# Loads, gains and first norms of the opening quads: which queue issues them and in which order

## The chip, the cores and the metric

The kernel runs on one core of one Trainium2 chip. A core has five engines with a queue of instructions each: TensorE (PE, matrix products and transposes), VectorE (DVE), ScalarE (ACT), GpSimd (POOL) and SyncE (SP, which here only issues DMA transfers). Every engine takes its own queue strictly in order and waits on semaphores for the others. The metric is device time in microseconds (us), the median of several executions. The profile is of one further execution.

## The reference

Attention with normalised queries and keys, followed by a feed-forward block with SoLU. The inputs are float32, but for the two weight matrices: these are float64, and the kernel reads them as pairs of 32-bit words.

```python
q_n = q / sqrt(mean(q*q, -1) + 1e-6) * g_q          # (8, 12, 448, 64); the same for k with g_k
scores = q_n @ k_n.T / 8
attn = exp(scores - max); attn = attn / (sum(attn) + 1e-9)
x = (attn @ v) as (3584, 768)
h = x @ w_in                                         # (768, 1024)
solu = h * softmax(h)
ln = (solu - mean) / sqrt(var + 1e-6) * g_ln
out = ln @ w_out                                     # (1024, 768)
```

## The kernel before

The 8 batches of 12 heads are 48 *pairs* of heads, and two pairs make a *quad*; there are 24 quads. The attention runs over them in one loop, with the order of every engine's work written out by hand (`tc.manual_schedule()`); the two products of the feed-forward block follow, with the block sums of a fast matrix multiplication. The change touches the set-up before the loop, and quad 0.

A quad m with pairs a and b goes through these steps. `scores(n, kc)` makes the scores for 128 of a pair's 448 keys on TensorE (L802) and an exponential `E` of them on ScalarE (L792), called E(n,kc) below; `scores_last(m)` does the remaining 64 keys of both pairs (L815). `add(n)` sums two of the exponentials on VectorE to `es` (L829). `values_last`, `values` multiply by v, `sums` makes the row sums of the exponentials on TensorE from `E` and `es` (L874), and `inverse` and `divide` end the quad on VectorE and GpSimd. Between them stand the preparations of later pairs: `squares` (ScalarE, L656), `row_sums` (VectorE, L664), `fold_one` or `fold_sums`, `rsqrt_seed` (Ln and Exp on ScalarE), `rsqrt_step` (four VectorE instructions of a Newton step), `normalise` (GpSimd, L713), `qk_transpose` (VectorE, L723) and `gain` (ScalarE, L727).

Pairs 0 and 1 are loaded by rows (`load_rows`, L738) and are transposed by TensorE: `square_rows` (L748, L750), `sum_rows` (L756), `rsqrt_seed`, `rsqrt_step` (L694 to L704), `normalise_rows` (the scaling, L764), `transpose_rows` (L770) and `take_rows` (L776, L778), the copy out of PSUM in which ScalarE multiplies q by the gain column `gcol`. All later pairs come through `load` (L634), eight transfers of 56 KB each. `load_gains` (L465 to L472) fetches the vectors g_q and g_k broadcast over the partitions (`gg`), once more as two rows, and g_ln (`grow`); `gain_columns` (L479 to L481) transposes the rows to `gcol` and multiplies the two broadcasts, `gain_limit` makes the factor of the q column from them.

The DMA transfers of both issuing queues take eight completion semaphores in turn, and each one waits until the transfer that last had its semaphore has landed. Before the loop SP issues, in this order: q of pair 0 (k goes over ScalarE's queue at the same time), the six transfers of the gains, pair 1, pair 2, v of quad 0, pairs 3, 4 and 5. In quad 0 SP goes on with v of quad 1 and pairs 6 and 7. Much later, in the first product of the feed-forward block, ScalarE's queue issues loads too (`load_x`, L924), and GpSimd's power serves the layer norm (L1050), one column at a time; L1052 is a scale and multiply of one column there.

Of the kernel before, what the change touches and what calls it, by code (L numbers as in the profile page):

```python
# [9 lines left out]
FP32 = mybir.dt.float32  # L10
# [4 lines left out]
OP = AluOpType  # L15
# [351 lines left out]
def fast_path(  # L367
# [24 lines left out]
    nc = tc.nc  # L392
    B, H, S, D = q.shape
    DM, DFF = moe_w_in.shape
    P = 128
    NJ = S // P
    NB = S // 32
# [64 lines left out]

    def load_gains():
        for i, g in enumerate((g_q, g_k)):
            nc.sync.dma_start(gg[:, i], g.rearrange("(o d) -> o d", o=1).to_broadcast([P, D]))  # L465
        for i, g in enumerate((g_q, g_k)):
            nc.sync.dma_start(
                grow[KF + i : KF + i + 1].rearrange("o (h d) -> o h d", h=2),
                g.rearrange("(o d) -> o () d", o=1).to_broadcast([1, 2, D]),
            )  # L470
        for i in range(2):
            nc.sync.dma_start(  # L472
                grow[i * HF : (i + 1) * HF].rearrange("c (g j) -> c g j", g=4),
                moe_g_ln.rearrange("(h g c j) -> h c g j", h=2, g=4, j=32)[i],
            )
# [148 lines left out]

    def load(n):
        b, hp = divmod(n, NP)
        h0 = 2 * hp
        d = st[n] = {}  # L630
        d["qk"] = loads.tile([P, 2, NB, 32], FP32, tag="qk", name="qk", bufs=5)
        for s, src in enumerate((q, k)):
            for g in range(4):
                nc.sync.dma_start(  # L634
                    d["qk"][g * 32 : g * 32 + 32, s],
                    src[b, h0 + g // 2].rearrange("(b t) (x d) -> x t b d", t=32, x=2)[g % 2],
                )
# [104 lines left out]
    def square_rows(n, s, engine):  # L742
        d = st[n]
        if s == 0:
            d["sq"] = xs.tile([P, 2, 4, P], FP32, tag="x", name="xsq")[0:R]
        x, y = d["qk"][:, s], d["sq"][:, s]
        if engine is nc.scalar:
            nc.scalar.activation(y, x, AF.Square)  # L748
        else:
            engine.tensor_tensor(y, x, x, OP.mult)  # L750

    def sum_rows(n, s):
# [4 lines left out]
            d["ss"][:, s * 8 : s * 8 + 8], d["sq"][:, s].rearrange("p j (h d) -> p (j h) d", h=2), AX, OP.add  # L757
        )

    def normalise_rows(n, s):  # L760
        d = st[n]
        x = d["qk"][:, s].rearrange("p j (h d) -> p (j h) d", h=2)
        y = d["y"][:, s * 8 : s * 8 + 8].rearrange("p i -> p i ()").to_broadcast([R, 8, D])
        nc.vector.tensor_tensor(x, x, y, OP.mult)  # L764
# [6 lines left out]

    def take_rows(n, s):
        d = st[n]
        if s == 0:
            d["qkT"] = work.tile([P, 2, S], FP32, tag="qkT", name="qkT", bufs=3)
            nc.scalar.activation(d["qkT"][:, 0], d["pt", 0], AF.Copy, scale=gcol[:, KF : KF + 1])  # L776
        else:
            nc.vector.tensor_copy(d["qkT"][:, 1], d["pt", 1])  # L778
# [524 lines left out]
    load_gains()  # L1303
    load_rows(1, (nc.sync, nc.sync, nc.sync, nc.sync))
    load(2)
    load_v(0)
    load(3)
    load(4)
    load(5)
    with tc.manual_schedule():  # L1310
        square_rows(0, 0, nc.vector)
        square_rows(0, 1, nc.scalar)
        sum_rows(0, 0)
        sum_rows(0, 1)
        rsqrt_seed(st[0])
        gain_columns()
        rsqrt_step(st[0])
        for s in range(2):
            normalise_rows(0, s)
            transpose_rows(0, s)  # L1320
        gain_limit()
        take_rows(0, 0)
        for s in range(2):
            square_rows(1, s, nc.scalar)
        take_rows(0, 1)
        for s in range(2):
            sum_rows(1, s)
        rsqrt_seed(st[1])
        rsqrt_step(st[1])
        for m in range(NQ):  # L1330
            a, b = 2 * m, 2 * m + 1

            def outputs():
                values_last(m)
                values(a)


            next1 = m + 1 < NQ
            next2 = m + 2 < NQ
            next3 = m + 3 < NQ  # L1340
            if m == 0:
                unit(lambda: scores(a, 0))
                normalise_rows(1, 0)
                normalise_rows(1, 1)
                unit(lambda: scores(a, 1))
                for s in range(2):
                    transpose_rows(1, s)
                    take_rows(1, s)
                squares(2)
                row_sums(2)  # L1350
                unit(lambda: scores(a, 2))
                fold_one(2)
                unit(lambda: scores_last(m))
                rsqrt_seed(norms["one", 2])
                rsqrt_step(norms["one", 2])
                normalise(2)
                add(a)
                unit(lambda: scores(b, 0))
                unit(lambda: scores(b, 1))
                unit(lambda: scores(b, 2))  # L1360
                squares(3)
                row_sums(3)
                qk_transpose(2)
                fold_one(3)
                gain(2)
                rsqrt_seed(norms["one", 3])
                add(b)
                rsqrt_step(norms["one", 3])
                normalise(3)
                load_v(1)  # L1370
                load(6)
                load(7)
                for _ in range(2):
                    load_next()
                unit(outputs)
                squares(4)
                row_sums(4)
                unit(lambda: values(b))
                squares(5)
                unit(lambda: sums(m))  # L1380
                inverse(m)
                qk_transpose(3)
                row_sums(5)
                fold_sums(2)
                later(1, lambda m=m: divide(m))
                continue
            early = 1 < m and next1
            if early:
                rsqrt_seed(norms[m + 1])
                rsqrt_step(norms[m + 1])  # L1390
                normalise(a + 2)
                normalise(b + 2)
            for x in joins_at.get(m, ()):
                combine_in(x)
            if next1:
                load_v(m + 1)
            unit(lambda: scores(a, 0))
            store_x(m - 1)
            if early:
                qk_transpose(a + 2)  # L1400
                if next3:
                    load(a + 6)
            unit(lambda: scores(a, 1))
            if m == 1:
                gain(b)
            unit(lambda: scores(a, 2))
            unit(lambda: scores_last(m))
            if m < 2:
                add(a)
            unit(lambda: scores(b, 0))  # L1410
            if m == 1:
                rsqrt_seed(norms[m + 1])
                rsqrt_step(norms[m + 1])
                normalise(a + 2)
                normalise(b + 2)
                load(a + 6)
                load(b + 6)
            unit(lambda: scores(b, 1))
            if early:
                qk_transpose(b + 2)  # L1420
                if next3:
                    load(b + 6)
            if m > 1:
                add(a)
            unit(lambda: scores(b, 2))
            if m == 1:
                qk_transpose(a + 2)
            scarce = m < 5
            if next2:
                squares(a + 4)  # L1430
                if not scarce:
                    squares(b + 4)
                row_sums(a + 4)
            if next1:
                gain(a + 2)
            if m == 1:
                add(b)
                qk_transpose(b + 2)
            if next1:
                gain(b + 2)  # L1440
            if scarce:
                squares(b + 4)
                if m > 1:
                    add(b)
            if next2:
                row_sums(b + 4)
                fold_sums(m + 2)
            if not scarce:
                add(b)
            add_more(a)  # L1450
            add_more(b)
            unit(outputs)
            step(m - 2)
            begin(m)
            step(m - 1)
            if m - 1 in sets:
                load_next()
            unit(lambda: values(b))
            if m == NQ - 1:
                block_sums(0, 0)  # L1460
                block_sums(0, 1)
                load_x(1)
            unit(lambda: sums(m))
            inverse(m)
            if next1:
                later(1, lambda m=m: divide(m))
            if m == NQ - 2:
                load_x(0)
                sizes(0)
# [191 lines left out]
```

## Time and profile before

| what | us |
|---|---|
| median of three runs | 823.76 (821.85 to 825.68) |
| the profiled execution | 826.51 |
| its span, first to last instruction | 824.4 |
| TensorE busy | 796.2 |
| VectorE, ScalarE, GpSimd busy | 673.0, 461.3, 462.3 |
| first product on TensorE starts | 7.88 |
| first scores start | 10.80 |

The span begins with the program's first instruction. "Busy" is the time in which an engine executes; issuing DMA transfers and waiting don't count. In the timeline, `ACTq` and `SPq` are the queues' own instructions, such as DMA issues; neighbouring instructions of one kind stand in one line with their count, and the duration then is that of all of them. What a wait is put down to is the semaphore that came last.

### The profile page before, as it was taken

The page shows a single profiled execution, that of the slowest core. Times are in us where ns is not written, and L with a number is a line of the kernel's source. Part 1 is how long each engine was busy: PE and PEld are TensorE (multiplying, and loading weights), DVE is VectorE, ACT ScalarE, POOL GpSimd, SP SyncE. Part 2 cuts the span into 40 slices and gives each one's busy share as a digit, 9 for nine tenths or more (in the row PEclk, how much of TensorE's full clock was granted, in tenths as well). Part 3 has the DMA queues.
Part 4 walks back from the last instruction along what each step waited for, and adds up shares of the span by engine and source line. Part 5 has one row for each costly group of instructions (what it writes and reads, how often), then busy time and mean ns, then how long its engine had stood idle before and what let it go on. Part 6 is the DMA issues. An engine that isn't in the chain of part 4 may idle for free.

```text
span 824.4 us, 14924 instructions
## 1 busy us (share of the span) xinstructions
PE 796.2 (97%) x5019; PEld 465.7 (56%) x5019; DVE 673.0 (82%) x1203; ACT 461.3 (56%) x755; POOL 462.3 (56%) x635
## 2 busy tenths in 40 slices
PE   5989999999999999999999999999889999999996
PEld 3333444344443443444444444444579999999996
DVE  6769897787878888589999999998896866866945
ACT  5668777676877777255665544452424464464420
POOL 1434555455555647322254368776487777877861
PEclk9999999999999999999999999999999999999999
DMA  6677877777677663325555534452447356476312
GB/s 120 119 190 154 186 178 167 180 139 172 145 181 181 131 144 117 101 78 148 157 152 145 134 100 117 135 156 64 142 153 268 128 208 223 137 237 203 123 58 82
DMA packets 272230, 122.81 MB, mean 149 GB/s; under 512 B 190736, under 2 KB 257296, under 8 KB 272144
## 3 DMA queue, kind: packets, MB, share of 16 engines
q1 hardware_dynamic: 257888, 112.09, 51.5%
q10 hardware_dynamic: 14256, 9.67, 4.2%
q8 instruction: 42, 0.69, 0.4%
q14 instruction: 44, 0.36, 0.1%
HBM read 85.01 MB, written 36.70 MB: 148 GB/s over the span
## 4 chain that ended last, share of the span: by engine, by line
PE 76%; SPq 9%; DMA 5%; DVE 3%; POOL 3%; ACT 2%; issue 2%; ACTq 0%; DVEq 0%; POOLq 0%
PE b L972 31%; PE A L1167 14%; PE o L855 8%; PE s L802 8%; SPq L634 8%; PE B L1167 7%; PE C L1167 3%; PE sm L874 3%; DMA v<-in_v_dram 2%; PE s L815 1%; PE o L844 1%; DMA qk<-in_k_dram 1%; ACT E L792 1%; DVE part L664 1%; POOL ss L674 1%
## 5 line engine op out<-in xcount | busy, mean ns | idle before, releaser
L972 PE MATMUL b<-w_in,xg 128*128 128x512 f32 x336 | 151.2, 592 | 0.0
L792 ACT ACTIVATE E<-s 128x896 f32<-128x896 f32 x168 | 138.9, 936 | 11.9 <-PE s L802 11.2
L802 PE MATMUL s<-qkT 64*64 64x448 f32 x1152 | 123.2, 554 | 1.4 <-DVE qkT L778 0.8
L972 PE MATMUL b<-w_in,xsum 128*128 128x512 f32 x252 | 115.0, 592 | 0.0
L855 PE MATMUL o<-E,v 128*64 128x448 f32 x576 | 113.5, 543 | 0.0
L972 PEld LDWEIGHTS b<-w_in,xg 128*128 128x128 f32 x336 | 63.8, 190 | 80.2 <-issue 76.4
L674 POOL COPY ss<-part 32x56 f32<-32x56 f32 x88 | 42.0, 477 | 103.8 <-DVE part L664 101.1
L713 POOL TENSOR_TENSOR qkn<-qk,ny 128x896 f32<-128x896 f32 x46 | 77.9, 1713 | 24.3 <-DMA qk<-in_k_dram 15.9
L1167 PE MATMUL A<-w_out,sums 128*128 128x192 f32 x392 | 80.1, 327 | 3.5 <-ACT u L1179 1.6
L802 PEld LDWEIGHTS s<-qkT 64*64 64x64 f32 x1152 | 47.5, 164 | 62.1 <-ACT E L792 30.7
L972 PEld LDWEIGHTS b<-w_in,xsum 128*128 128x128 f32 x252 | 47.9, 190 | 60.3 <-issue 57.6
L1050 POOL TENSOR_TENSOR he<-he,mhalf 128x1 f32<-128x1 f32 x28 | 17.0, 608 | 114.6 <-DVE he L1049 112.5
L1167 PE MATMUL B<-w_out,sums 128*128 128x192 f32 x392 | 79.9, 326 | 1.2 <-DVE P L1211 1.2
L855 PEld LDWEIGHTS o<-E,v 128*64 128x64 f32 x576 | 39.2, 137 | 72.6 <-issue 66.8
L1056 ACT ACTIVATE u<-u,shift,he 128x1024 f32<-128x1024 f32 x28 | 34.7, 1240 | 74.6 <-POOL shift L1052 74.6
L1167 PEld LDWEIGHTS A<-w_out,sums 128*128 128x128 f32 x392 | 66.0, 190 | 4.9 <-issue 1.8
L1167 PEld LDWEIGHTS B<-w_out,sums 128*128 128x128 f32 x392 | 66.1, 190 | 1.7 <-DVE P L1211 1.5
L664 DVE TENSOR_REDUCE part<-sq 128x28 f32<-128x896 f32 x46 | 49.1, 1083 | 15.8 <-ACT sq L656 14.0
L829 DVE TENSOR_TENSOR es<-E 128x896 f32<-128x896 f32 x48 | 52.6, 1097 | 0.5 <-ACT E L792 0.5
L563 POOL TENSOR_TENSOR w_out<-w_out 128x384 f32<-128x384 f32 x44 | 50.7, 1158 | 1.9
L656 ACT ACTIVATE sq<-qk 128x896 f32<-128x896 f32 x46 | 43.9, 984 | 13.1 <-DMA qk<-in_k_dram 10.5
L723 DVE STREAM_TRANSPOSE qkT<-qkn 128x896 f32<-128x896 f32 x46 | 48.9, 1094 | 1.9 <-POOL qkn L713 1.8
(136 smaller groups left out, 1489.8 us busy)
## 6 DMA issues: line engine op xcount, KB each, us to landing
ur<-ud SPq DMA_DIRECT2D x60, 256.0 KB, 4.1
ud<-ub SPq DMA_DIRECT2D x112, 128.0 KB, 2.2
xd<-xo SPq DMA_DIRECT2D x24, 448.0 KB, 3.4
qk<-in_q_dram SPq DMA_DIRECT2D x184, 56.0 KB, 2.3
qk<-in_k_dram SPq DMA_DIRECT2D x184, 56.0 KB, 2.1
v<-in_v_dram SPq DMA_DIRECT2D x24, 384.0 KB, 4.8
out_dram<-P SPq DMA_DIRECT2D x21, 384.0 KB, 2.6
raw<-in_moe_w_in_dram SPq DMA_DIRECT2D x12, 512.0 KB, 4.8
```

Of the source, the lines that this page charges most:

```text
L563: nc.gpsimd.tensor_tensor(o, p, q, OP.subtract)
L634: nc.sync.dma_start(d["qk"][g * 32 : g * 32 + 32, s], src[b, h0 + g // 2].rearrange("(b t) (x d) -> x t b d", t=32, x=2)[g % 2],)
L664: nc.vector.tensor_reduce(norms[m]["part"][:, i], st[n]["sq"], AX, OP.add)
L674: e.tensor_copy(ss[g * 32 : g * 32 + 32], part[o * 32 : o * 32 + 32])
L713: e.tensor_tensor(d["qkn"], d["qk"].rearrange("p s b d -> p (s b) d"), y.rearrange("p b -> p b ()").to_broadcast([P, 2 * NB, 32]), OP.mult,)
L723: nc.vector.transpose(d["qkT"].rearrange("p s t -> p (s t)"), d["qkn"].rearrange("p b d -> p (b d)"))
L792: nc.scalar.activation(d["E", kc], s[:, :, 0:S], AF.Exp)
L802: nc.tensor.matmul(s[c : c + D, h, 0:S], d["qkT"][hh, 1, keys], d["qkT"][hh, 0, :], start=True, stop=True,)
L829: nc.vector.tensor_tensor(d["es"], d["E", 0], d["E", 1], OP.add)
L855: nc.tensor.matmul(d["o"][h * D : (h + 1) * D, :], quads[n // 2]["v"][:, n % 2 * 2 + h, kc], d["E", kc][:, h], start=False, stop=(kc == NJ ...
L972: nc.tensor.matmul(o, a[:, c], w_in[i][:, c], start=(c == 0), stop=(c == HD - 1))
L1167: nc.tensor.matmul(k[bank], a[:, c].rearrange("p a i -> p (a i)"), w_out[:, area, i, c], start=begin and c == 0, stop=c == KC - 1, skip_gr ...
```

## The change

- `load_gains` issues its six transfers on ScalarE's queue instead of SP's.
- Before the loop, SP loads pair 3 ahead of v of quad 0. Pair 5 is no longer loaded there: in quad 0, after the exponential of `scores(b, 2)` and ahead of `squares(3)`, ScalarE's queue issues its eight transfers.
- For pairs 0 and 1, `rows_power` takes the place of `rsqrt_seed` and `rsqrt_step`: one VectorE instruction for mean + 1e-6, and GpSimd's power with the exponent -0.5.
- `warm_up` runs first: VectorE clears a tile, and TensorE multiplies it with itself six times. Nothing reads the result.
- The squares of pair 1 stand before the scalings of pair 0, the sum of its q squares before `gain_limit`, and k is copied out of PSUM ahead of q.

```diff
 def load_gains():
     for i, g in enumerate((g_q, g_k)):
-        nc.sync.dma_start(gg[:, i], g.rearrange("(o d) -> o d", o=1).to_broadcast([P, D]))
+        nc.scalar.dma_start(gg[:, i], g.rearrange("(o d) -> o d", o=1).to_broadcast([P, D]))
...
-    def load(n):
+    def load(n, queue=nc.sync):
...
-                nc.sync.dma_start(
+                queue.dma_start(
...
+    def rows_power(n):
+        d = st[n]
+        y = d["y"] = small.tile([P, 4 * NB], FP32, tag="ny", name="ny", bufs=2)[0:R, 0:16]
+        nc.vector.tensor_scalar(y, d["ss"], 1.0 / D, 1e-6, OP.mult, OP.add)
+        nc.gpsimd.tensor_tensor(y, y, mhalf[0:R].to_broadcast([R, 16]), OP.pow)
+
+    def warm_up():
+        w = work.tile([P, 2, S], FP32, tag="r", name="warm", bufs=1)[:, 0]
+        nc.vector.memset(w[:, 0:S], 0.0)
+        o = ps_t.tile([P, S], FP32, tag="o", name="pt", bufs=2)
+        for _ in range(6):
+            nc.tensor.matmul(o, w[:, 0:P], w[:, 0:S], start=True, stop=True)
...
     load(2)
+    load(3)
     load_v(0)
-    load(3)
     load(4)
-    load(5)
     with tc.manual_schedule():
+        warm_up()
         square_rows(0, 0, nc.vector)
         square_rows(0, 1, nc.scalar)
         sum_rows(0, 0)
         sum_rows(0, 1)
-        rsqrt_seed(st[0])
+        rows_power(0)
         gain_columns()
-        rsqrt_step(st[0])
+        for s in range(2):
+            square_rows(1, s, nc.scalar)
         for s in range(2):
             normalise_rows(0, s)
             transpose_rows(0, s)
+        sum_rows(1, 0)
         gain_limit()
+        take_rows(0, 1)
         take_rows(0, 0)
-        for s in range(2):
-            square_rows(1, s, nc.scalar)
-        take_rows(0, 1)
-        for s in range(2):
-            sum_rows(1, s)
-        rsqrt_seed(st[1])
-        rsqrt_step(st[1])
+        sum_rows(1, 1)
+        rows_power(1)
...
                 unit(lambda: scores(b, 2))
+                load(5, nc.scalar)
                 squares(3)
```

More of the change, by code (lines that the diff above doesn't have):

```diff
@@ L464, in load_gains @@
         for i, g in enumerate((g_q, g_k)):
-            nc.sync.dma_start(gg[:, i], g.rearrange("(o d) -> o d", o=1).to_broadcast([P, D]))
+            nc.scalar.dma_start(gg[:, i], g.rearrange("(o d) -> o d", o=1).to_broadcast([P, D]))
         for i, g in enumerate((g_q, g_k)):
-            nc.sync.dma_start(
+            nc.scalar.dma_start(
                 grow[KF + i : KF + i + 1].rearrange("o (h d) -> o h d", h=2),
@@ L471, in load_gains @@
         for i in range(2):
-            nc.sync.dma_start(
+            nc.scalar.dma_start(
                 grow[i * HF : (i + 1) * HF].rearrange("c (g j) -> c g j", g=4),
@@ L633, in load @@
             for g in range(4):
-                nc.sync.dma_start(
+                queue.dma_start(
                     d["qk"][g * 32 : g * 32 + 32, s],
@@ L773, in take_rows @@
         d = st[n]
+        if "qkT" not in d:
+            d["qkT"] = work.tile([P, 2, S], FP32, tag="qkT", name="qkT", bufs=3)
         if s == 0:
-            d["qkT"] = work.tile([P, 2, S], FP32, tag="qkT", name="qkT", bufs=3)
             nc.scalar.activation(d["qkT"][:, 0], d["pt", 0], AF.Copy, scale=gcol[:, KF : KF + 1])
```

## The prediction

> **What bounds the kernel now.** I read the page first: TensorE (PE) fills the span.
>
> ```profile
> span 824.4 us, 14924 instructions
> PE 796.2 (97%) x5019; PEld 465.7 (56%) x5019; DVE 673.0 (82%) x1203; ACT 461.3 (56%) x755; POOL 462.3 (56%) x635
> ```
>
> So only the 28 us in which TensorE is idle can be won, and whatever makes it wait is lost in full. The change touches the first quads, so next come TensorE's waits up to 80 us.
>
> ```profile
> PE pg L479 <- DMA grow<-in_moe_g_ln_dram: 7.9, 1, 7.9
> PE s L815 <- ACT E L792: 3.6, 3, 1.6
> PE s L802 <- DVE qkT L778: 0.8, 1, 0.8
> PE s L802 <- DVE r L885: 0.6, 1, 0.6
> PE s L815 <- ACT qkT L727: 0.4, 1, 0.4
> ```
>
> After the start of 7.9 us only 5.4 us of waiting is left; from 62.3 us on TensorE hardly stops, so what stands there goes through to the end. Third, the timeline (start, duration, engine, line, operation; in brackets the idle time before it and its releaser), for the start and for the end of quad 0:
>
> ```profile
> 1.70 0.49 SPq L465 DMA_DIRECT2D gg<-in_g_q_dram  x1
> 4.54 0.63 ACT L748 ACTIVATE xsq<-x 112x512 f32<-112x512 f32 x1 [2.54 <-DMA x<-in_k_dram]
> 7.49 1.42 DVE L764 TENSOR_TENSOR x<-x,ny 112x512 f32<-112x512 f32 x2
> 10.80 3.27 PE L802 MATMUL s<-qkT 64*64 64x448 f32 x16 [0.81 <-DVE qkT L778]
> ...
> 19.32 2.51 ACT L792 ACTIVATE E<-s 128x896 f32<-128x896 f32 x3
> 21.71 0.96 ACT L656 ACTIVATE sq<-qk 128x896 f32<-128x896 f32 x1
> 22.71 1.09 DVE L664 TENSOR_REDUCE part<-sq 128x28 f32<-128x896 f32 x1 [1.62 <-ACT sq L656]
> 23.78 2.05 SPq L634 DMA_DIRECT2D qk<-in_q_dram  x4
> 25.71 1.08 DVE L829 TENSOR_TENSOR es<-E 128x896 f32<-128x896 f32 x1
> 29.77 0.95 ACT L656 ACTIVATE sq<-qk 128x896 f32<-128x896 f32 x1 [2.35 <-DMA qk<-in_k_dram]
> 31.58 0.97 PE L815 MATMUL s<-qkT 64*64 64x448 f32 x4 [1.56 <-ACT E L792]
> ```
>
> SP issues without a pause, about 0.52 us a load (2.05 for four), and pair 5's land last: ScalarE waits 2.35 us for them, and TensorE 1.56 for ScalarE. The second thing to see is the chain squares(3) 21.71, row_sums(3) 22.71, add(b) 25.71 to 26.79: TensorE reaches the sums with that `es` at about 26.8. It has no slack.
>
> Two more lines carry the argument: SP's waits up to 20 us, and ScalarE at 407 us.
>
> ```profile
> SPq L738 <- DMA gg<-in_g_q_dram: 1.4, 1, 1.4
> ...
> 407.81 1.15 ACT L1032 ACTIVATE u<-h,hmax 128x1024 f32<-128x1024 f32 x1 [0.21 <-DVE hmax L1026]
> 407.82 1.74 ACTq L924 DMA_DIRECT2D xg<-xd  x2
> 409.60 0.59 ACT L983 COPY q<-b 128x512 f32<-128x512 f32 x1 [0.55 <-issue]
> ```
>
> The first: in the built program the DMAs take eight completion semaphores in turn, and each waits for the landing of the one that had its semaphore before. The second: ScalarE issues DMAs while an activation runs, but what follows in its queue starts only after the last issue (409.56).
>
> **What the Trainium skill says.** "DMA: Bandwidth & Descriptors", Issuing engines are not separate DMA queues: a second issuing engine saves only sequencer time, the transfers share the same 16 engines. The trace agrees: rows from SP and ScalarE, issued side by side at 0.72 and 0.75, were ready together (4.18, 4.54). "TensorE: Matmul & The Clock Gate", Part 1: TensorE runs at half rate until about 3.4 us of activity, and falls back after such a stretch of idleness. The trace agrees on the first: the sets of score products up to 13.8 us come 0.747 us apart, later ones 0.376. Part 4 of that page says that transposes don't count as activity; here they ran from 8.24 to 9.99, and the products after them were still slow. "GPSIMD Engine Reference", section 3.1, gives about 2.6 cycles for each column of an ordinary two-input operation (2.2 ns at the 1.2 GHz of its section 1); 896 columns took 1.71 us here, somewhat less. It gives no price for the power.
>
> **The change, part by part.**
>
> *Gains on ScalarE.* Removed from SP: six issues from 1.70 to 4.90 and the 1.4 us wait. Added to ScalarE: the same six, ahead of pair 0's k square. The built program shows that the last of them waits for g_q's broadcast, which took 5.01 us from issue. Its issue stays at about 1.7, so it lands near 6.7; ScalarE is free at about 7.1 and not 4.54. With square 0.63, sum 0.64 and small gaps the sums are complete at 8.4 (before: 6.18).
>
> *Power.* Before, Ln, Exp and four VectorE steps took 1.27 us (6.18 to 7.45). Now one VectorE step (0.17), about 0.15 us of handing over, and a 112x16 power on GpSimd. The trace has only 128x1 powers: 0.542 us at best, 0.948 the first. Bounds: 0.54 if columns are free; 4.8 if each costs what the one-column power costs over the one-column scale and multiply (0.55-0.265 = 0.28, times 16, plus 0.265). Below nothing is excluded for the operation; the exchange itself can gain 0.4. I take 1.2: the first-use value and 16 columns at the ordinary price, rounded up, since 56 ordinary columns cost 0.302. Then 1/rms is there at 9.95 (before 7.45), two scalings 1.42, the sum of pair 1 that now stands ahead 0.64, the gain steps 0.77, the copy 0.63: scores start at about 13.45, not 10.80: **+2.65**. The gain columns arrive at about 9 (last gain issue 6.75 plus 2.1), which this hides.
>
> *Pair 1* then needs k copy, sum (to 13.95), step, power (to 15.4), scalings 1.3, transposes 0.75: third scores at 17.6 instead of 15.76. Its squares are done in ScalarE's idle time and its Ln and Exp are gone, so the lag is **+1.9** there.
>
> *Six products of zeros.* The memset and they lie in TensorE's idle start; at 0.747 us each they end near 5.7. From there to 13.45 TensorE has only the gain transpose and the row transposes, so I expect it at half rate again: 0. If it stayed at full rate, four sets at 0.37: -1.5 at most, and about -0.5 after ScalarE's chain. They can't cost: nothing waits for them.
>
> *Order of loads.* SP starts pair 1 at once, then four of pair 2's eight issues wait for gain transfers; pair 2 is issued by 10.7 instead of 12.3, pair 3 ahead of v. The v load moves from 12.3 to about 15 and is needed at 20: hidden, cost 0; without cover it would be those 2.5 us.
>
> *Pair 5 on ScalarE.* Eight issues stand behind E(b,2) and ahead of squares(3). 8 x 0.52 = 4.16, less 0.83 that the exponential covers, plus a small gap: squares(3) is late by **3.5**. Behind it wait row_sums(3), the transposition of pair 2, fold_one(3) and add(b) on VectorE, and then TensorE, in the sums: +3.5 in full, because there is no slack.
>
> *Given back.* Pair 5 has landed when ScalarE asks for it, so the 1.57 wait goes: **-1.6**. The 0.39 behind it hangs on the transposition of pair 3 and stays. The waits of quad 2 (0.59 and 1.65, at 45.3 and 46.9) end a chain from Ln at 35.57 over GpSimd's scalings, VectorE and the fold back to ScalarE at 47.6; it keeps its length: 0. The 0.41 at 61.9 follows a transfer (ScalarE waited 1.9 us for pair 9), and SP is ahead by then: **-0.4**.
>
> *Extras.* After a wait of over 3.4 us TensorE may start slowly again: 0.5 (up to four sets at 0.37, part of it hidden by the exponentials). SP's issues sometimes take longer (3.07 for four at 18.58): on ScalarE I add 0.5.
>
> Sum: 1.9+3.5-1.6-0.4+1.0 = **+4.4** us. The profiled execution took 826.51 (span 824.4 and 2.1 around it), so 830.9 for such a one; against the median of 823.76, **828.2**. A measurement of this kernel can tell about 0.5% (4.1 us) from no change: the forecast lies just outside.
>
> **Rivals.** (a) *The lag is absorbed.* ScalarE is 56% busy, and quad 2's 2.2 us of waits may shrink by 1 to 2 once pair 5 is early; without the extras that leaves +1 to +2.5: about 825.5. Against it: quad 2's chain names GpSimd and VectorE, no transfer. (b) *Power is dear.* At 4.8 us both pairs' chains grow by 3.6 each, +7.2 on top: 835.4; at 2.5 us 830.8. For it: 0.28 us of the one-column power is unexplained. Against: a one-off part is as likely. (c) *Loads decide* (faster). If ScalarE's issues hid behind its queued exponentials, the 3.5 would go, and with SP some 8.8 us lighter (3.2+1.4+4.2) all waits after 29 us could go: 1.9-4.6-1.5 = -4.2, 819.6. It decides if add(b) ends within about 0.5 us of TensorE's arrival at the sums. Against it stands the 409.60 line.
>
> **Numbers.** Forecast 0.58 (own range 825.5 to 831), (a) 0.15, (b) 0.16, (c) 0.11. Slower by over 0.5% (above 827.9): a little over half of the forecast and all of (b), 0.50; faster (below 819.6) 0.11; between them 0.39. The range leaves out the far halves of (b) and (c): 820.5 to 835.
>
> **What would show it.** ScalarE's first square near 7.1; first scores near 13.4 and 0.75 us apart; eight issues on ScalarE's queue from about 23 to 27; a wait of 3 to 4 us before the sums with `es`; none for pair 5. A square at 5, a power under 0.7, or an `es` in time would make this too slow a forecast; a power over 2 us too fast a one.

## The result and the profile after

| | before | after |
|---|---|---|
| median, us | 823.55 (821.85 to 825.68, four runs) | 831.71 (830.22 to 834.5, four runs) |
| the profiled execution, us | 826.51 | 831.87 |
| its span, us | 824.4 | 829.8 |

The changed kernel is slower: its time is 1.0102 of that before, 95% interval 1.0066 to 1.0137. That is 8.2 us between the medians and 5.4 us between the two profiled executions. The profiled execution before lies some 1.3 us above what the same kernel takes in longer series (825.2 us, median of 38 runs), so lags that are read between the two profiles come out a little small at the end.

The head of the page of the kernel after:

```profile
span 829.8 us, 14926 instructions
PE 804.4 (97%) x5031; PEld 471.5 (57%) x5031; DVE 669.9 (81%) x1198; ACT 459.4 (55%) x751; POOL 468.8 (56%) x637
```

TensorE is busy for 8.2 us more, 7.5 of which are the products of zeros (1.37 to 8.87). Nearly all of that lies in time that was idle before (up to 7.88 us), and it is no loss by itself. The waits of TensorE up to 80 us (total, times, longest) say more:

```profile
PE pt L784 <- DVE x L778: 5.1, 2, 3.9
PE sm L889 <- DVE es L844: 2.8, 1, 2.8
PE s L830 <- ACT E L807: 1.7, 1, 1.7
PE pt L772 <- DVE warm L769: 1.4, 1, 1.4
PE pg L479 <- DMA grow<-in_moe_g_ln_dram: 0.8, 1, 0.8
PE s L817 <- ACT qkT L791: 0.8, 1, 0.8
PE s L817 <- DVE r L900: 0.6, 1, 0.6
```

Two of the longer ones are new. Both row transposes wait for the scaling, which waits for 1/rms (3.9 and 1.3 us), and the sums wait for `es` (2.8). Of the old ones, the 1.56 us for pair 5 is gone; quad 2's 0.59 and 1.65 are still there (0.6 and 1.7). The timeline of the kernel after (start, duration, engine, line, operation, idle time before) shows where they come from:

```profile
6.79 0.58 ACTq L467 DMA_DIRECT2D grow<-in_g_k_dram  x1
7.41 0.78 ACTq L472 DMA_DIRECT2D grow<-in_moe_g_ln_dram  x2
8.30 0.63 ACT L748 ACTIVATE xsq<-x 112x512 f32<-112x512 f32 x1 [6.29 <-DMA qk<-in_q_dram]
9.94 2.92 POOL L764 TENSOR_TENSOR ny<-ny,mhalf 112x16 f32<-112x16 f32 x1 [8.03 <-DVE ny L763]
12.90 1.41 DVE L778 TENSOR_TENSOR x<-x,ny 112x512 f32<-112x512 f32 x2 [3.04 <-POOL ny L764]
16.32 3.27 PE L817 MATMUL s<-qkT 64*64 64x448 f32 x16 [0.81 <-ACT qkT L791]
17.06 2.92 POOL L764 TENSOR_TENSOR ny<-ny,mhalf 112x16 f32<-112x16 f32 x1 [1.72 <-DVE ny L763]
...
29.63 2.08 ACTq L634 DMA_DIRECT2D qk<-in_k_dram  x4
31.89 0.95 ACT L656 ACTIVATE sq<-qk 128x896 f32<-128x896 f32 x1 [3.02 <-DMA qk<-in_k_dram]
35.87 1.08 DVE L844 TENSOR_TENSOR es<-E 128x896 f32<-128x896 f32 x1
37.01 0.58 PE L889 MATMUL sm<-es,ones 128*32 128x224 f32 x8 [2.76 <-DVE es L844]
```

ScalarE's first square stands behind the issues of the gains until 8.30 us; each power takes 2.92 us; the first scores start at 16.32, 5.5 us later than before; the squares of pair 3 stand behind pair 5's eight issues (27.28 to 31.71).

The lag of TensorE, read as the start of the same matmul in both traces: 5.5 us at the first scores, 6.8 at the third scores, 10.2 at the sums on `es`, 11.6 and 10.0 at the matmuls that stood at 29.0 and 31.6 us before (40.6 and 41.6 after), 10.35 at the one that stood at 62.3, 6.3 at the one at 320, and 5.6 at the end. From here on, a lag "at 62 us" or "at 320 us" is that of the matmul that stood there in the kernel before. So about 10 us are lost in the first 62 us, and 4 come back by 320. A hint of where they come back is the chain that ended last, by engine, first of before, then of after:

```profile
PE 76%; SPq 9%; DMA 5%; DVE 3%; POOL 3%; ACT 2%; issue 2%; ACTq 0%; DVEq 0%; POOLq 0%
```

```profile
PE 89%; DVE 3%; POOL 2%; issue 2%; DMA 2%; ACT 1%; ACTq 0%; DVEq 0%; POOLq 0%
```

Before, 14% of the chain is SyncE's issuing and the transfers; after, 2%. In the stretch from 60 to 330 us of the kernel before, ScalarE waits for loads (the waits of ScalarE there):

```profile
ACT sq L656 <- DMA qk<-in_k_dram: 6.3, 5, 2.5
...
ACT sq L656 <- DMA v<-in_v_dram: 1.3, 1, 1.3
```

In the kernel after there is none of these. In this execution the kernel before was held up by its loads in the middle of the attention, and the changed kernel, whose TensorE comes later, meets them landed.

The rest of the early loss is the clock. The busy times of the kernel after by stretch; the third column from the end is the granted clock of TensorE:

```profile
13.70:23.90 10.20, 8.07 (x40) 4.18 (x44) 5.59 (x12) 3.94 (x5) 3.14 (x2) 0.50 0.70 136
24.00:37.60 13.60, 10.84 (x112) 4.29 (x104) 7.52 (x23) 7.71 (x13) 2.48 (x1) 1.00 0.44 81
37.70:41.00 3.30, 3.30 (x20) 1.12 (x23) 3.14 (x6) 1.70 (x3) 2.46 (x5) 0.50 0.69 111
41.10:58.00 16.90, 14.65 (x136) 5.99 (x128) 11.55 (x22) 10.31 (x17) 6.55 (x16) 1.00 0.75 177
58.10:61.50 3.40, 3.40 (x20) 1.15 (x24) 3.30 (x6) 2.60 (x4) 3.28 (x2) 0.50 0.65 167
```

Three stretches ran at half rate: the first scores and the start of the third (to 23.96 us; the kernel before had full rate from 15.58 us on), 3.4 us behind the wait for `es`, and 3.4 us behind quad 2's waits. They took the lag from 6.8 to 7.4 us, from 10.2 to 11.7, and from 9.4 to 10.9. The kernel before had the same waits in quad 2 and stayed at full rate there; the last section shows why.

### The profile page after: what moved, and what is told of

Same layout as the page of the kernel before. It is cut to its first block, busy times and chain, and to the rows that moved or that the text cites. A ratio compares the mean times of both kernels' runs of the same rounds, so it can differ in the third digit from the quotient of the medians.

```text
span 829.8 us, 14926 instructions
## 1 busy us (share of the span) xinstructions
PE 804.4 (97%) x5031; PEld 471.5 (57%) x5031; DVE 669.9 (81%) x1198; ACT 459.4 (55%) x751; POOL 468.8 (56%) x637
## 4 chain that ended last, share of the span: by engine, by line
PE 89%; DVE 3%; POOL 2%; issue 2%; DMA 2%; ACT 1%; ACTq 0%; DVEq 0%; POOLq 0%
PE b L987 30%; PE A L1182 14%; PE s L817 13%; PE o L870 12%; PE B L1182 7%; PE sm L889 5%; PE C L1182 3%; PE s L830 2%; PE o L859 2%; DMA v<-in_v_dram 1%; POOL ny L764 1%; POOL sums L1161 0%; ACT E L807 0%; DMA qk<-in_k_dram 0%; POOL sums L1160 0%
## 5 line engine op out<-in xcount | busy, mean ns | idle before, releaser
L817 PE MATMUL s<-qkT 64*64 64x448 f32 x1152 | 125.0, 562 | 1.4 <-ACT qkT L791 0.8
L817 PEld LDWEIGHTS s<-qkT 64*64 64x64 f32 x1152 | 49.3, 165 | 62.2 <-ACT E L807 27.0
L1182 PE MATMUL A<-w_out,s 128*128 128x192 f32 x224 | 45.7, 326 | 0.8 <-ACT u L1194 0.8
```

The source lines that it names most:

```text
L817: nc.tensor.matmul(s[c : c + D, h, 0:S], d["qkT"][hh, 1, keys], d["qkT"][hh, 0, :], start=True, stop=True,)
L1182: nc.tensor.matmul(k[bank], a[:, c].rearrange("p a i -> p (a i)"), w_out[:, area, i, c], start=begin and c == 0, stop=c == KC - 1, skip_gr ...
```

## The experiments

The theory: three parts lose time, each by what it puts ahead of TensorE's chain (power, gains on ScalarE, pair 5 on ScalarE), the products of zeros and the other order do nothing, and the waits for loads of the kernel before take up a part of the lag. The rivals: one part alone carries it, so that undoing another gives nothing; or the reordering costs something; or the half rate is the cause and not a consequence. Each ratio is to the kernel before, on the same chip and beside it.

**1. The changed kernel without the power.**

```diff
-        rows_power(0)
+        rsqrt_seed(st[0])
         gain_columns()
+        rsqrt_step(st[0])
 ...
-        rows_power(1)
+        rsqrt_seed(st[1])
+        rsqrt_step(st[1])
```

> The changed kernel with Ln, Exp and the four VectorE steps back for pairs 0 and 1 instead of the power. Theory (power, gains on ScalarE and pair 5 on ScalarE each cost their own part): the profile shows 2.92 us per power and 1.27 for the old steps in the kernel before; first scores about 1.9 us earlier than in the changed kernel (14.4 instead of 16.3), third scores about 3 earlier (19.5 instead of 22.5), time 3 us below the changed kernel, about 828.7. Rival (the power's time is hidden, because ScalarE's late squares and the loads set the pace anyway): less than 1 us gained, 831.

828.29 us, ratio 1.0042 (1.0026 to 1.0058). The row transposes lag by 3.25 us in place of 5.5, the lag at 62 us is 4.55 in place of 10.35. The wait for `es` is a little longer than in the changed kernel, which shows that it isn't the power's (TensorE's waits up to 80 us, the two longest):

```profile
PE sm L889 <- DVE es L844: 3.3, 1, 3.3
PE pt L784 <- DVE x L778: 1.9, 1, 1.9
```

**2. The changed kernel with pair 5 issued by SyncE ahead of the loop again.**

```diff
     load(4)
+    load(5)
 ...
-                load(5, nc.scalar)
                 squares(3)
```

> The changed kernel with pair 5 issued by SP before the loop again. Theory: ScalarE's squares(3) follow the exponential at once, TensorE's wait of 2.8 us before the sums with es and the half-rate stretch after it go; 3 to 4 us below the changed kernel, about 828. Rival (SP's lead is worth as much): SP loses 4.2 us of lead, waits for pair 5 and later pairs come back as in the kernel before, no more than 1 us gained, 831.

829.07 us, 1.0057 (1.0033 to 1.0080): the theory, give or take 1 us. The wait for `es` is gone and no half rate follows; the lag at 62 us is 6.0. What is left are the two waits for the power and the squares:

```profile
PE pt L784 <- DVE x L778: 5.1, 2, 3.8
```

**3. The changed kernel with the gains issued by SyncE again.**

```diff
-            nc.scalar.dma_start(gg[:, i], ...)
+            nc.sync.dma_start(gg[:, i], ...)
```

(and the other four of `load_gains` likewise)

> The changed kernel with the six gain transfers on SP's queue again. Theory: ScalarE's first square at 4.5 and not 8.3 us, first scores at about 12.6 and not 16.3; SP's loads 3 to 4 us later, which pair 5 on ScalarE and the late start still hide; 2.5 us below the changed kernel, about 829.2. Rival (the start is absorbed later): within 1 us of the changed kernel, 831.7.

830.43 us, 1.0075 (1.0046 to 1.0104), between the two. The first scores start at 12.76 us and not at 16.32, so the part costs 3.6 us at its place. But TensorE, coming earlier, then waits longer for `es`, and runs at half rate for 6.8 us behind that (33.3 to 40.1) in place of 3.4; at 62 us it is 6.4 us late. TensorE's waits:

```profile
PE sm L889 <- DVE es L844: 4.8, 1, 4.8
```

The squares of pair 3 hang on more than TensorE's progress: SyncE is later again by the six issues, and pair 5's four k loads on ScalarE took 3.43 us in this run (2.08 in the changed kernel).

**4. The changed kernel without the products of zeros.**

```diff
-        warm_up()
         square_rows(0, 0, nc.vector)
```

> The changed kernel without the six products of zeros and their memset. Theory: nothing, 831.7 within 1 us: the records show the full rate from 6.9 to 13.7 us only, before the first scores at 16.3. Rival (the products are worth something, or they do harm by shifting the stretches of half rate at 37.6 and 58.1): 1.5 us or more away on either side.

832.25 us, 1.0095 (1.0067 to 1.0124). The products give nothing and cost nothing.

**5. The changed kernel with three parts undone:** the edits of 1, 2 and 3 together. The order of loads, the products of zeros and the moved squares, sums and copies stay.

> The changed kernel with three of its parts undone: the g vectors on SyncE again, 1/rms by the Ln, Exp and VectorE steps again, pair 5 issued by SyncE ahead of the loop. The other order of loads, the products of zeros and the moved takes, squares and sums stay. Theory (the three parts carry the whole loss, and their shares of 0.6, 0.45 and 0.27% overlap a little): as the kernel before, 822 to 825 us, first scores at 10.8 us, no hold of the half sums es. Rival (the reordering itself costs something, which the single undoings could not show): 826 to 828 us, with the first or third scores over 1 us later than in the kernel before.

826.29 us, 1.0012 (0.9996 to 1.0027), where the kernel before took 825.2. The first scores start at 11.94 us, 1.1 later than before, behind a wait of 2.4 us for q's copy, ahead of which pair 1's squares and k's copy now stand; and the third scores are 1.1 us late too. By its time and by these 1.1 us that is what the rival had said: the reordering does cost something at its place. But the lag is gone at the place where the kernel before waits for pair 5 (-0.1 at 31.6 us); the 1.0 us at 62 us come from half rate behind quad 2's waits, and 0.1 is left at 320. The three parts hold the loss, but for about 1 us that can't be told from none.

**6. The changed kernel with pair 5's issues one place later.**

```diff
-                load(5, nc.scalar)
                 squares(3)
+                load(5, nc.scalar)
```

> The changed kernel with pair 5's issues put behind quad 1's squares instead of ahead of them, still on ScalarE. Theory (the loss of this part is that the squares, and behind them es, wait for 4.4 us of issues): es is on time, the wait of the sums for es falls from 2.8 to under 0.5 us, no half rate after it, and the 4 us of issues fall into idle time of ScalarE: 828 to 829.5 us, as with pair 5 on SyncE. Rival (ScalarE has no room anywhere in that stage: what follows the squares is late instead): 831 to 832.5 us, with a wait of over 2 us for ScalarE or VectorE in the next 8 us.

829.67 us, 1.0052 (1.0031 to 1.0072): the theory, 0.2 us above its range. TensorE doesn't wait for `es`, as if SyncE had issued the pair (2), and the lag at 62 us is 6.2. So it isn't the issuing on ScalarE that costs, but that squares which TensorE's chain hangs on stand behind it.

**7. The changed kernel with six more products of zeros, behind the gain transposes.**

```diff
         gain_columns()
+        for _ in range(6):
+            nc.tensor.matmul(wo, ww[:, 0:P], ww[:, 0:S], start=True, stop=True)
         for s in range(2):
             square_rows(1, s, nc.scalar)
```

> The changed kernel with six more products of zeros behind the gain transposes, in TensorE's idle time ahead of the row transposes (12 matmuls of 0.31 us at full rate, 3.8 us; 7.5 us at half rate). The output does not depend on them. Theory (the full rate lapses because TensorE is idle from 8.9 to 14.3 us): no stretch of half rate between 10 and 24 us, the first 16 products of scores take 3.3 us less in sum by 24 us; some of it goes into longer waits for the loads and for es, 829 to 830.5 us. Rival (what TensorE gains early it waits for later, as the first run without the products of zeros suggests): 831 to 832.5 us, with the sums on es no earlier.

832.91 us, 1.0089 (1.0062 to 1.0116): the rival, 0.4 us above its range. The granted clock from 10 to 20 us is 0.99 in place of 0.69, and TensorE makes up 1.9 us within the first scores (lag 6.0 at the row transposes, 4.1 at the matmul of 13.07 us before). It then waits 2.8 us for pair 1's scaling, in place of 1.3, runs at 0.67 from 20 to 30 us, and reaches the sums on `es` 10.9 us late, no earlier than without them (10.2). At this place TensorE isn't the bound: pair 1's chain over the power is.

**8. The kernel before with the power alone.** The edit is that of 1, the other way round.

> The kernel before with one part of the change: 1/rms of the first two pairs by GpSimd's power. Theory (SyncE issues 12.6 us of loads for each quad of 12.9 us, and TensorE loses about 5 us to late loads between 60 and 330 us; a lag of TensorE alone falls into those waits first): first scores 1.8 to 2 us later, third scores 3 to 4 us later, but the end within 1.5 us of the kernel before: 824 to 826.5 us, with the waits of the squares for loads shrunk. Rival (the parts add, as the undoing of this part gave 3.4 to 5 us): 827.5 us or more.

826.12 us, 1.0002 (0.9991 to 1.0013), beside 825.91 for the kernel before. The power takes 2.92 us here too, and the lag is 2.7 us at 62. By 259 us it is gone: -0.2. Of the 6.3 us for which ScalarE's squares waited for k loads, 0.4 are left.

**9. The kernel before with pair 5 on ScalarE alone.** The edit is that of 2, the other way round.

> The kernel before with one part of the change: pair 5 issued by ScalarE ahead of quad 1's squares. Theory: the sums wait 2.5 to 3.5 us for es, half rate for a while after it, and SyncE runs 4 us ahead, so that the waits of the squares for loads go; lag and lead cancel for the most part: 824 to 827 us. Rival (the parts add; the undoing of this part gave 3.8 us): 827.5 to 829.5 us.

825.35 us, 0.9997 (0.9982 to 1.0012). The hold is there (TensorE's waits up to 80 us):

```profile
PE sm L874 <- DVE es L829: 3.3, 1, 3.3
```

The lag rises to 3.5 us there, by another 1.3 at half rate, and falls by 1.9 where the wait for pair 5 was; at 62 us it is 2.0. From 60 to 330 us no square waits for a load.

**10. The kernel before with the gains on ScalarE alone.** The edit is that of 3, the other way round.

> The kernel before with one part of the change: the g vectors' six loads issued by ScalarE. Theory (a lag of TensorE up to some 2.5 us falls into the waits for loads, what is above it stays): the first scores 3 to 4 us later than 10.8, about 3 us of lag left at 60 us, 824 to 827 us. Rival (this part alone is already over what the waits can take, and a stretch of half rate comes with it): 827.5 us or more.

824.88 us, 0.9996 (0.9982 to 1.0011), beside 824.79. The row transposes lag by 3.1 us, at 62 us it is 2.7, at 320 -1.3.

Three parts that measure as nothing alone make 1% together. The traces say why. In the profiled execution of the kernel before, TensorE loses 4.0 us between the matmuls at 62 and at 320 us: 1.9 in four waits, the rest in matmuls around them that count as busy. The changed kernel and those of runs 1 to 4, 9, 10 and 12 gain 4.02 to 4.04 us on it between the same two matmuls, whatever their lag: but for 0.3 us in run 4, no square of theirs waits for a load there any more. A lag of 2 to 3 us at 62 us is repaid in this way in runs 8 to 10. What is above 4.0 stays: the changed kernel's 10.35 becomes 6.3, the 4.55, 6.0 and 6.4 of runs 1 to 3 become 0.5, 2.0 and 2.4 (in medians, which stand against a kernel before that is usually a little faster than its profiled execution, 3.5, 4.3 and 5.6). Lag alone isn't enough to meet the loads landed, though: in runs 5, 6, 7, 8 and 11 squares still wait for loads there, and only 0.9, 1.6, 3.3, 2.6 and 1.3 us come back. In run 6 these waits are 5.6 us, in spite of 6.2 us of lag. Why SyncE is that late there is left open. The 4.0 us are those of one execution, too, which was 1.3 us slower than the median.

**11. The gains issued by GpSimd,** in the kernel before.

```diff
-            nc.sync.dma_start(gg[:, i], ...)
+            nc.gpsimd.dma_start(gg[:, i], ...)
```

> The kernel before with one edit: the six loads of the g vectors issued by GpSimd in place of SyncE. Theory (the loss of this part in the change is ScalarE's, whose first square stands behind the issues; SyncE without them is some 4 us ahead, and the later waits for late rows go): first scores within 0.5 us of 10.8, pair 1's rows 2 us earlier, the waits of ScalarE's squares for loads between 64 and 300 us shrink from 6.3 us, 820.5 to 823 us. Rival (GpSimd's queue is slower to issue, and the gain columns come late): first scores at 12 us or later, 825 us or more.

824.94 us, 0.9997 (0.9983 to 1.0010). The rival: the gain columns come 2.6 us and the first scores 2.4 us later (13.2). But the lag is 0.5 at 62 us, and the waits of the squares for k loads shrink to 3.1 us. SyncE's earlier start, by six issues once, brings no gain; what it seems to lack is time in every quad, which the next run tests.

**12. Two loads of every quad issued by GpSimd,** in the kernel before: `vl` and the raw rows of w_in.

```diff
-            nc.sync.dma_start(to, w[c * P : (c + 1) * P])
+            nc.gpsimd.dma_start(to, w[c * P : (c + 1) * P])
 ...
-            nc.sync.dma_start(d["vl"][i * D : (i + 1) * D], ...)
+            nc.gpsimd.dma_start(d["vl"][i * D : (i + 1) * D], ...)
```

SyncE's queue in a quad of the kernel before (timeline, SyncE alone):

```profile
87.04 1.98 SPq L634 DMA_DIRECT2D qk<-in_q_dram  x4
89.06 2.04 SPq L634 DMA_DIRECT2D qk<-in_k_dram  x4
91.15 0.48 SPq L510 DMA_DIRECT2D raw<-in_moe_w_in_dram  x1
91.72 0.38 SPq L647 DMA_DIRECT2D v<-in_v_dram  x1
92.15 2.21 SPq L651 DMA_DIRECT2D vl<-in_v_dram  x2
94.46 0.54 SPq L906 DMA_DIRECT2D xd<-xo  x1
95.11 2.33 SPq L634 DMA_DIRECT2D qk<-in_q_dram  x4
```

There is hardly a gap: from one store of `xo` to the next it is 12.5 to 12.7 us of issues in these two quads (81.73, 94.46, 106.97), against 12.9 us of TensorE for a quad. A queue that is that full can hardly catch up.

> A candidate to beat both, and a test of what paces the kernel before: the kernel before with two loads of every quad, vl (two of 32 KB) and w_in's raw rows, issued by GpSimd in place of SyncE. SyncE's issues for a quad fall from 12.6 to about 10.9 us, against 12.9 us of TensorE. Theory (loads pace the stretch from 60 to 330 us): the waits of the squares for loads go, and 820 to 822 us. Rival (GpSimd's queue, in order, holds ss and qkn behind issues that wait for buffers): 825 us or more, with waits for POOL ss or qkn.

822.96 us beside 825.91 for the kernel before, 0.9968 (0.9957 to 0.9978): the theory, 1 us above its 820 to 822, and the fastest of all kernels here. From 60 to 330 us TensorE is busy throughout; first this kernel, then the kernel before:

```profile
60.00:330.00 270.00, 270.00 (x2672) 113.42 (x2664) 227.67 (x354) 203.02 (x291) 179.22 (x285) 1.00 0.71 159
```

```profile
60.00:330.00 270.00, 267.69 (x2619) 109.57 (x2613) 225.72 (x352) 203.66 (x291) 148.55 (x237) 1.00 0.72 160
```

GpSimd's busy time grows by 31 us, and hardly anything waits longer for it (ScalarE 44.0 us for `ss` in place of 42.2). The kernel's lag is 0.7 us at 62 and -3.35 at 320: the same 4.0 us. This is what the loads cost the kernel before in its profiled execution; between the medians it is 3.0 us, by the ratio 2.6.

## Why the prediction was right

It said slower, 828.2 us with a range to 835, and it was 831.7. The sum was +4.4 us, against 5.4 between the profiled executions and 8.2 between the medians. Three of its terms were far off, in opposite directions: the start (6.8 us at the third scores for 1.9), half rate (3.0 behind the waits for 0.5), and what comes back late (4.0 for nothing).

- **Gains on ScalarE**: mechanism right, size short. The first square came at 8.30 and not at 7.1. The prediction let the last issue wait for g_q's broadcast; the one that held longest was an earlier one, of g_k's row: the semaphore that it takes is that of a transfer of pair 1's rows, issued by SyncE at 1.70, and it began only at 6.79. The eight semaphores go round over both queues together. Run 3 has this part at 3.6 us where it stands.
- **Power**: a mis-sized term. Taken as 1.2 us within bounds of 0.54 and 4.8, it is 2.92 us, twice: columns do cost, about 0.16 us each over the one-column power of 0.54. With the square (1.2 us) and one power (1.7) the first scores come 2.9 us later than forecast (16.32 against 13.45), with the second power the third scores 4.9 later (22.5 against 17.6).
- **Products of zeros**: 0, as run 4 shows. The full rate that they released lapsed before the first scores, as expected. They ended at 8.87 rather than 5.7: the matmuls are twelve, not six, since each float32 product is two here.
- **Order of loads**: 0 was right within 0.3%, together with the products of zeros and the moved squares, sums and copies (run 5).
- **Pair 5**: mechanism right, and the size where it stands alone: 3.5 us in run 9. In the changed kernel the lag rises by 3.4 from the third scores to the sums, but 0.7 of that are scores at half rate and 2.8 the wait for `es`. Run 6 shows that it hangs on the place of the issues in ScalarE's queue.
- **Given back, early**: the 1.6 us came (11.56 to 9.97), and quad 2's two waits stayed, as forecast. The 0.39 behind pair 5, which was to stay, went too (9.97 to 9.43).
- **Given back, late**: the 0.4 at 61.9 us came (10.94 to 10.35). Nothing was forecast beyond, and 4.0 came between 62 and 320 us. The prediction read the waits only up to 80 us, and took it that TensorE hardly stops after 62. TensorE's own waits further on are four of 0.3 to 0.7 us; ScalarE's for loads, shown above, are longer.
- **Extras**: right in kind (half rate after the wait), 0.5 against 3.0 us: 1.5 behind the wait for `es`, and 1.5 in a second such stretch behind quad 2's waits. Both hang on where these waits fell, as the last section shows.

At the matmul of 62 us the forecast was 4.4 us of lag against 10.35; the late return, which it did not have, covered 4.0 us of the difference. So the direction and the mechanisms of the loss were right, but that the time came out so near is in part luck: errors of opposite sign cancel. Of the rivals, the dear power had part of the truth (2.92 lies between its 2.5 and its 4.8), and "the lag is absorbed" is what happens to a part of it, though at the loads and not in quad 2. That loads decide was right for the kernel before, but with pair 5 alone (run 9) the two effects cancel, and only run 12 gains from it.

The Trainium skill, "TensorE: Matmul & The Clock Gate", Part 1, has the clock fall back after some 3.4 us of idleness. Here waits of 2.76 us, and of 0.59 and 1.66 close together, were followed by half rate, so the traces show it on less than that in one piece; the last section shows what counts in them.

## What to carry to other kernels

An engine that waits at two places in turn, at the start for a chain and later for its loads, can repay a small lag: parts that measure as nothing alone can then add up to a loss, so an undoing and a doing alone are both needed. Ask of each issuing queue how many microseconds of issues it has for each turn of the loop; at 12.6 of 12.9 us it is the bound to relieve: two or three issues fewer in every turn gained 3.0 us (run 12), six fewer at the start nothing (run 11). Before giving loads to a computing engine, see what stands behind them in its queue: the same eight issues cost 3.5 us ahead of the squares (run 9), and nothing that shows behind them (run 6 against run 2).

## What the hardware showed unexpectedly

- The granted clock changes on a grid of 3.41 us. In all 14 traces each stretch between two changes is a whole number of 3.41 us long: the changed kernel has 2, 3, 4, 1, 5, 1 and 224 of them. The grid begins at another place in each trace, 0.1 to 2.8 us after the first instruction. The 7.5 us of products of zeros brought full rate from 6.9 to 13.7 us; from 10.3 to 13.7 TensorE did nothing, and half rate followed.
- It isn't the length of a wait that decides about half rate, but TensorE's busy share within one cell of the grid. Over the 14 traces, half rate followed on all 30 cells at full rate with a share under 0.40, and on none of the 3262 with 0.49 or more; of the seven cells between, it followed on two. Full rate followed on all 31 cells at half rate with a share over 0.82, and on none of the 52 under 0.77 (the stretch ahead of the first change counts as half rate). So it is luck whether a wait that is shorter than a cell costs half rate: an edge may divide it. These are the cells with quad 2's waits (length, then TensorE's busy time), first in the changed kernel, then in the kernel before:

```profile
54.69:58.10 3.41, 1.16 (x16) 0.37 (x16) 1.96 (x8) 1.55 (x4) 2.06 (x10) 1.00 0.63 105
```

```profile
42.89:46.30 3.41, 2.82 (x36) 1.13 (x32) 1.74 (x3) 1.51 (x2) 0.57 (x3) 1.00 0.98 330
46.30:49.71 3.41, 1.76 (x20) 0.48 (x16) 2.04 (x7) 2.60 (x5) 2.53 (x8) 1.00 0.80 160
```

In the first, both waits lie in one cell, with a share of 0.34; in the second, an edge at 46.30 us divides them into 0.83 and 0.52. Half rate came behind them in runs 5, 7, 10 and 12 too (0.30 to 0.48), and not in the other eight. The waits for `es` of runs 1 and 7 (3.3 and 2.4 us) were divided as well, and full rate stayed.
- GpSimd's power on 112x16 takes 2.92 us in every run, ScalarE's Ln and Exp on the same tile 0.31 and 0.22.
